# Where the DMAs of an attention and expert kernel are issued: puts of p back to SP, some loads of u to GpSimd, and the last chunk and the tails spread otherwise

## The chip, the cores and the metric

The kernel runs on one core of a Trainium2 chip. The metric is the time of one execution on the device, in microseconds (us). Engines are named as in the profile: PE (TensorE matmuls), PEld (its weight loads), DVE (VectorE), ACT (ScalarE), POOL (GpSimd), SP (SyncE, which here does nothing but issue DMAs). A "q" behind an engine's name (SPq, ACTq) is its sequencer, which waits and issues DMAs.

## The reference

Three stages over u, v (8 x 3072 x 256) and z (8 x 3072 x 64), all float32:

```python
scores = z @ z.T / 3072                   # per batch, 3072 x 3072, symmetric
attn   = maximum(scores, 0) ** 2
x      = u * (attn @ v)                   # 24576 rows of 256
h      = x @ w_in                         # 1024 wide
solu   = h * softmax(h)
ln     = (solu - mean) / sqrt(var + 1e-6) * g_ln
x2     = ln @ w_out                       # 256 wide
expert = argmax(x2 @ w_gate)              # 8 experts, one for each row
out[row] = gate * (maximum(x2 @ w1[e], 0) @ w2[e])
```

## The kernel before

**Tiling.** Each batch's 3072 rows are cut into 6 chunks of 512 rows, 48 chunks in all, and the keys of a batch into 24 blocks of 128. One *slot* is one key block of one chunk, so a chunk has 24 slots and the attention has 1152. In a slot PE multiplies one block of squared scores (128 x 512, kept as a high part `ah` and a rest `al`) with v by six matmuls into `o`. Every float32 product is made of three passes (`mm3`: L108, L109, L110).

**Symmetry.** Because the scores are symmetric, a block is computed once. Its transposed copy is written to DRAM (`kept<-sym`, `kept<-a`, L399) and fetched back when the chunk of the other side needs it (`sym<-kept`, L406: four DMAs of 64 KB for a block). So chunk 0 of a batch computes all its 24 blocks, chunk 1 20, chunk 2 16, chunk 3 12, chunks 4 and 5 8 each; the others are fetched. In chunk 5 the four blocks 16 to 19 are computed again rather than fetched. A fetched block is either transposed by DVE (`a<-sym`, L412) or read directly by ACT (`ah<-sym`, L438). ACT makes `ah`, DVE makes `al` (L443), and PE uses both. `order(j, end)` gives the order of the blocks in a chunk: the fetched ones ("old") and the others ("new") are spread evenly among each other.

**The blocks of p.** Behind the attention, each chunk has four pieces of 128 rows (t = 0..3) that go through the SoLU part in the slots of the next chunks: matmul `h`, exponential, product `p`, a 32 x 32 block transpose on DVE into `pb` (L527), then `blk_put` (L536: four DMAs of 128 KB from SBUF to the DRAM tensor `moved`), `blk_get` (L542: four DMAs that bring it back as `pT`), `blk_split` (`pth`, `ptl`), the matmuls `yp`, and `y` (L565, DVE). In each slot window of a chunk four such pieces pass. A chain of small operations (`blk_scale`, `blk_logits`, `blk_route`; mostly POOL and DVE in turn) finds each row's expert and position, and four indirect DMAs from POOL (`blk_scatter`, L659) write the rows to `sorted_rows`.

**Order.** The program is written out by hand: `at(slot, fn, ...)` puts a step into a slot, and for every slot the steps are emitted in turn. Each engine then works through its own list in that order. SP's list holds the loads of u (`load_u`, L328: two DMAs of 64 KB in each of the slots 2 to 5 of a chunk), of v and z, the fetches, the puts and gets of p, and later the experts' weights (L811) and rows (L805). In slot n, SP is given the fetch for the block of slot n + 7.

**Semaphores of DMAs.** The DMAs that SP and ACT issue share eight completion semaphores (101 to 106, 108, 109 in the trace) in the order of the program; a DMA that takes a semaphore first waits until the DMA that had it before has landed, whichever of the two engines issued that one. POOL's DMAs have eight others (111 to 118).

**Experts.** From slot 1152 on (called NS), rows are taken from `sorted_rows` in units of 512 or 256 with their expert's weights, which are split into high parts and rests (L816, L817). The units that need only the rows of the first 44 chunks begin at NS, beside the pieces of p of the last chunks. `take` gives SBUF of the attention to the experts; `split_w`, `load_w` and `load_x` prepare the first unit in the slots of the last chunk (s0 is its first slot).

In the kernel before, `blk_put` is issued from ACT when its slot lies in the window of chunk 4 or 5 of a batch (except for the last chunk's own pieces), and from SP in all others. The functions that the change touches:

Of the kernel before, what the change touches and what calls it, by code (L numbers as in the profile page):

```python
# [33 lines left out]
def attention_moe_kernel(ctx, tc, u, v, z, w_in, w_out, g_ln, w_gate, w1, w2, out):  # L34
    nc = tc.nc
# [8 lines left out]
    NCB = S // CH  # L44
    NKB = S // P
    NCHUNK = B * NCB
# [6 lines left out]
    PD = 1  # L53
    ZL = 8
    XA, XT0, XE = 2, 21, 23
    SA, SB, SC, SD, SH = 11, 14, 16, 19, 1
    TW = 8
    WS, W0, W1, W2 = 4, -11, 0, 2
    YT = 1
# [41 lines left out]
    V, A, G, T = nc.vector, nc.scalar, nc.gpsimd, nc.tensor  # L101
# [30 lines left out]
    with ExitStack() as st:  # L132
# [22 lines left out]
        def at(slot, fn, *args):  # L155
            events[slot].append((fn, args))

        def after_them(slot, fn, *args):

            events_after[slot].append((fn, args))  # L160
# [3 lines left out]
        t = vp.tile([P, 2, 4, D], F32R, tag="vw", name="raw64").bitcast(I32).rearrange("p a r d -> p (a r d)")  # L164
        raw64 = [t[:, i * 2 * CH:(i + 1) * 2 * CH].rearrange("p (f two) -> p f two", two=2) for i in range(2)]
        t = mp.tile([P, F], F32, tag="pT", name="cu64").bitcast(I32)
        c64, u64 = t[:, :CH], t[:, CH:]
        t = [mp.tile([P, CH], F32R, tag=k, name="t64").bitcast(F32) for k in ("pth0", "ptl0", "pth1", "ptl1")]
# [94 lines left out]
        z_raw, v_raw, u_raw = {}, {}, {}  # L263
        z_t, z2_t, v_t = {}, {}, {}

        def rows(x, c):
            b, j = divmod(c, NCB)
            return x[b, j * CH:(j + 1) * CH]
# [54 lines left out]
        def load_u(c, x):  # L323
            if x == 0:
                u_raw[c] = raw.tile([P, KD, CH], F32, tag="ur", name="ur")
            src = rows(u, c).rearrange("(a i) (k b j) -> k b i a j", i=32, b=4, j=32)
            for k in range(KD):
                nc.sync.dma_start(out=u_raw[c][x * 32:(x + 1) * 32, k].rearrange("i (a j) -> i a j", j=32), in_=src[k, x])  # L328

# [2 lines left out]
        def again(q, k):  # L334
            return q == NCB - 2 and k == NCB - 1
# [11 lines left out]
        t = [xrow.tile([P, KD * CH], F32, tag="x", name="sym") for _ in range(2)]  # L347
        t = [x[:, i * CH:(i + 1) * CH] for x in t for i in range(2)]
# [3 lines left out]
        def order(j, end=False):  # L352


            old = [kb for kb in range(4 * j) if end or not again(kb // 4, j)]
            new = [kb for kb in range(NKB) if kb not in old]
            return [kb for _, kb in sorted([((i + 0.5) / len(old), kb) for i, kb in enumerate(old)] +
                                           [((i + 0.5) / len(new), kb) for i, kb in enumerate(new)])]

        orders = [order(c % NCB, c == NCHUNK - 1) for c in range(NCHUNK)]  # L360

        def block(n):
# [167 lines left out]

        moved = [nc.dram_tensor(f"moved_{i}", (32, 4, F), F32, kind="Internal").ap() for i in range(4)]

        def blk_put(c, t, eng):
            w = pb_t.pop((c, t))
            for x in range(4):
                eng.dma_start(out=moved[t][:, x], in_=w[x * 32:(x + 1) * 32])  # L536

        def blk_get(c, t):
            pT_t[c, t] = w = mp.tile([P, F], F32, tag="pT", name="pT")
# [299 lines left out]
        for i in range(NU):  # L839
            w = HALF if i < N_CUT else units[i]  # L840
# [71 lines left out]
        for c in range(NCHUNK):  # L912
            b, j = divmod(c, NCB)
            s0 = c * NKB
            sb = b * NCB * NKB
            if b == 0:
                base = 4 * j - Z0
                zload = base - 5 + (j > 0)
                vload = 4 * j - V0
                at(base, turn_z, c)  # L920
            else:

                late = j >= NCB - 2
                base = sb + 3 + 4 * (j - NCB + 2) if late else sb - (NCB - 1 - j) * NKB + ZB
                zload = base - (4 if late else ZL)
                vload = sb - NKB + VL + VS * j
                at(base - 2, turn_z, c)
            at(zload, load_z, c)
            at(base, prep_z, c)
            if c > 0:  # L930
                at(s0 - LA - 5, swap_z, c)
            for h in range(2):
                step, wait = (3, 5) if b else (2, 2)
                at(vload + step * h, load_v, c, h)
                at(vload + step * h + wait, prep_v, c, h)
                at(vload + step * h + wait + (b > 0), prep_v_lo, c, h)
            for x in range(4):
                at(s0 + 2 + x, load_u, c, x)
            at(s0 + 14, turn_u, c)

            last = c == NCHUNK - 1
            more = 2 if last else 1
            s1 = s0 + NKB
            for t in range(4):
                w = s1 + 2 + (TW if last else 6) * t
                at(w, blk_h, c, t, 0)
                at(w + 1, blk_h, c, t, 1)
                at(w + 1, blk_max, c, t)
                after_them(w + 2, blk_exp, c, t)
                at(w + 3, blk_mul, c, t)  # L950
                at(w + 4, blk_turn, c, t)
                at(w + 6, blk_var, c, t)

                out_, back, cut_, y = (4, 6, 10, 12) if last else (5, 8, 12, 15) if c < NCHUNK - 2 else (5, 7, 9, 12)

                at(w + out_, blk_put, c, t, nc.scalar if (w + out_) // NKB % NCB >= NCB - 2 and not last else nc.sync)
                at(w + back, blk_get, c, t)
                cut_, y = w + cut_, w + y
                at(cut_, blk_split, c, t, 0)
                at(cut_ + 1, blk_split, c, t, 1)  # L960
                at(y, blk_y, c, t, 0)
                at(y + 1, blk_y, c, t, 1)
            e = y + 3
            for i in range(3):
                at(e + more * i, blk_scale, c, i)
            for i in range(2):
                at(e + more * (3 + i), blk_scale, c, 3)
            at(e + more * 5, blk_logits, c)
            for i in range(10):
                at(e + more * (6 + i + 2 * (i > 5)), blk_route, c, i)  # L970
            for t in range(4):
                at(e + more * (6 + 2 * t), blk_rows, c, t)
                at(e + more * (18 + 2 * t), blk_scatter, c, t)
        after = e + more * 24
        for b in range(n_in + n_out):
            for i in range(14):
# [15 lines left out]
        s0 = NS - NKB  # L992
        at(s0, take, "raw1")
        at(s0, load_w, 0, 1)
        at(s0 + 5, take, "w1h")
        at(s0 + 10, take, "w1l")
        at(s0 + 14, take, "raw2")
        at(s0 + 14, load_w, 0, 2)
        at(s0 + 19, take, "xT0")
        at(NS, take, "w2h")  # L1000
        at(NS, take, "hT")
        at(NS, take, "w2l")
# [40 lines left out]
        with tc.manual_schedule():  # L1043
            for n in range(min(lo_slot, -LA), hi_slot + 1):
                i = n + LA
                k = n - NS
# [61 lines left out]
```

## Time and profile before

| | us |
|---|---|
| median of 3 runs | 4489.14 |
| lowest and highest | 4488.82, 4499.24 |
| the profiled execution's own time | 4495.23 |
| span of the profiled execution (first to last instruction) | 4493.5 |
| PE busy, share of the span | 4293.5, 96% |
| DVE, ACT, POOL busy, share of the span | 71%, 62%, 25% |
| mean granted TensorE clock | 0.981 |

[...] In the list of waits, each row says which instruction waited for which, the total, how often and the longest. In the view by windows, each row is a stretch of time from the span's start, with the busy time of each engine in it.

### The profile page before, as it was taken

How to read it: one execution, taken by the hardware profiler on the slowest of the kernel's cores; microseconds unless marked ns; L12 is line 12 of the kernel's file. 1: busy time of each engine (PE TensorE's matmuls, PEld its weight loads, DVE VectorE, ACT ScalarE, POOL GpSimd, SP SyncE). 2: the span in 40 equal slices, each digit the busy share in tenths (PEclk: the TensorE clock that was granted, in tenths of full speed). 3: DMA queues.
4: the chain of work that ended last, by engine and by line, in shares of the span. 5: the costliest groups of instructions: out<-in, count | busy, mean ns of one | idle time of the engine just before them, and what ended most of it. 6: DMA issues, size and time to landing. Idle time of an engine off the chain costs nothing. (4 is left out here: it accounts for less than half of the span.)

```text
span 4493.5 us, 74098 instructions
## 1 busy us (share of the span) xinstructions
PE 4293.5 (96%) x23458; PEld 3701.0 (82%) x23458; DVE 3200.8 (71%) x5624; ACT 2797.7 (62%) x5184; POOL 1123.2 (25%) x2358
## 2 busy tenths in 40 slices
PE   7999998999899999999999999999789999999998
PEld 5877887888788788878877887887678999999998
DVE  8767776777687677768767776777556755666686
ACT  6756775776577577658756765875444444444565
POOL 5022222322222232222223222322122211111112
PEclk9999999999999999999999999999889999999999
DMA  5887787778778778877887887778665655555575
GB/s 151 172 154 150 182 177 137 173 175 164 140 188 176 141 177 175 162 145 181 170 151 173 171 169 143 176 168 157 119 143 141 162 141 141 141 141 142 154 214 164
DMA packets 2529034, 719.20 MB, mean 160 GB/s; under 512 B 2326653, under 2 KB 2417021, under 8 KB 2528640
## 3 DMA queue, kind: packets, MB, share of 16 engines
q1 hardware_dynamic: 2497248, 629.76, 66.7%
q0 software_dynamic: 19104, 51.15, 3.3%
q10 hardware_dynamic: 12288, 33.57, 2.8%
q8 instruction: 183, 3.00, 0.3%
q14 instruction: 211, 1.73, 0.1%
HBM read 442.46 MB, written 273.49 MB: 159 GB/s over the span
## 5 line engine op out<-in xcount | busy, mean ns | idle before, releaser
L109 PE MATMUL o<-al,vw 128*128 128x512 f32 x2304 | 931.8, 404 | 136.9 <-DVE al L443 136.4
L108 PE MATMUL o<-ah,vw 128*128 128x512 f32 x2304 | 922.6, 400 | 4.5 <-DVE ut L467 4.4
L110 PE MATMUL o<-ah,vw 128*128 128x512 f32 x2304 | 915.1, 397 | 0.0
L438 ACT ACTIVATE ah<-a 128x512 fp32r<-128x512 f32 x832 | 525.6, 632 | 199.0 <-DVE a L412 95.2
L109 PEld LDWEIGHTS o<-al,vw 128*128 128x128 f32 x2304 | 442.8, 192 | 250.8 <-DVE al L443 172.6
L428 ACT ACTIVATE r<-s 128x512 f32<-128x512 f32 x704 | 414.6, 589 | 376.8 <-PE s L423 359.3
L433 ACT ACTIVATE a<-r 128x512 f32<-128x512 f32 x704 | 438.5, 623 | 238.2 <-issue 101.6
L443 DVE TENSOR_TENSOR al<-a,ah 128x512 fp32r<-128x512 f32 x832 | 577.5, 695 | 1.2 <-ACT ah L438 0.3
L110 PEld LDWEIGHTS o<-ah,vw 128*128 128x128 f32 x2304 | 443.3, 192 | 94.4
L108 PEld LDWEIGHTS o<-ah,vw 128*128 128x128 f32 x2304 | 441.6, 192 | 91.2 <-DVE ut L467 5.9
L105 DVE TENSOR_TENSOR ptl<-pT,pth 128x512 fp32r<-128x512 f32 x384 | 264.9, 690 | 328.3 <-ACT pth L104 327.2
L108 PE MATMUL yp<-gw,pth 128*128 128x264 f32 x1536 | 445.0, 290 | 0.4 <-ACT pth L104 0.4
L109 PE MATMUL yp<-gw,pth 128*128 128x264 f32 x1536 | 443.9, 289 | 0.0
L110 PE MATMUL yp<-gw,ptl 128*128 128x264 f32 x1536 | 442.9, 288 | 0.2 <-DVE ptl L105 0.2
L865 ACT ACTIVATE zw_x<-g 128x512 fp32r<-128x512 f32 (+1 forms) x350 | 182.6, 522 | 402.9 <-PE g L110 392.4
L866 DVE SCALAR_TENSOR_TENSOR zw_x<-g,zw_x 128x512 fp32r<-128x512 f32 (+1 forms) x350 | 208.2, 595 | 266.5 <-ACT zw_x L865 261.3
L108 PEld LDWEIGHTS yp<-gw,pth 128*128 128x128 f32 x1536 | 296.3, 193 | 16.6 <-ACT pth L104 0.6
L109 PEld LDWEIGHTS yp<-gw,pth 128*128 128x128 f32 x1536 | 296.6, 193 | 15.6
L659 POOL DMA_INDIRECT sorted_rows<-y,pi x192 | 205.6, 1071 | 402.6 <-DMA sorted_rows<-y,pi 330.8
L491 PE MATMUL h<-w_in,xt 128*128 128x512 f32 x768 | 305.5, 398 | 0.0
L490 PE MATMUL h<-w_in,xt 128*128 128x512 f32 x768 | 305.3, 398 | 0.0
L110 PEld LDWEIGHTS yp<-gw,ptl 128*128 128x128 f32 x1536 | 296.0, 193 | 0.6 <-DVE ptl L105 0.6
(275 smaller groups left out, 10520.7 us busy)
## 6 DMA issues: line engine op xcount, KB each, us to landing
vw_x<-in_moe_w SPq DMA_DIRECT2D x124, 1024.0 KB
sym<-kept SPq DMA_DIRECT2D x1792, 64.0 KB
pT<-moved SPq DMA_DIRECT2D x768, 128.0 KB
kept<-sym SPq DMA_DIRECT2D x320, 256.0 KB
moved<-pb SPq DMA_DIRECT2D x512, 128.0 KB
kept<-a SPq DMA_DIRECT2D x128, 256.0 KB
moved<-pb ACTq DMA_DIRECT2D x256, 128.0 KB
vr<-in_v SPq DMA_DIRECT2D x96, 256.0 KB
```

The lines of the kernel that those rows point to most:

```text
L105: V.tensor_tensor(out=lo, in0=src, in1=hi.bitcast(F32), op=ALU.subtract)
L108: T.matmul(out=out, lhsT=lh, rhs=rh, start=start, stop=False, **kw)
L109: T.matmul(out=out, lhsT=lh, rhs=rl, start=False, stop=False, **kw)
L110: T.matmul(out=out, lhsT=ll, rhs=rh, start=False, stop=stop, **kw)
L428: A.activation(out=r, in_=s_t.pop(n), func=AF.Relu)
L433: A.activation(out=a, in_=r_t.pop(n), func=AF.Square)
L438: A.activation(out=h, in_=a_t[n], func=AF.Copy)
L443: V.tensor_tensor(out=l, in0=a_t[n], in1=ah_t[n].bitcast(F32), op=ALU.subtract)
L490: T.matmul(out=h[:, fs], lhsT=w[:, 0, kd, ts_], rhs=w_in_t[0][:, kd, fs], start=(kd == 0), stop=False)
L491: T.matmul(out=h[:, fs], lhsT=w[:, 0, kd, ts_], rhs=w_in_t[1][:, kd, fs], start=False, stop=False)
L659: G.indirect_dma_start(out=xs[:DUMMY], out_offset=bass.IndirectOffsetOnAxis(ap=pi[:, t:t + 1].bitcast(U32), axis=0), in_=y_t[c][:, t, :], ...
L866: V.scalar_tensor_tensor(out=lo, in0=h, scalar=0.0, in1=hi.bitcast(F32), op0=ALU.max, op1=ALU.subtract)
```

## The change

1. All puts of p are issued from SP, those in the windows of chunks 4 and 5 too (before: from ACT).
2. `load_u` of chunks 4 and 5 of every batch is issued from POOL's queue (before: SP).
3. In the very last chunk, `order` puts the chunk's own four blocks last, and the four blocks that are computed again are spread among the 16 fetched ones, which so take 20 slots. The steps that take over the SBUF of v and the split of the first unit's w1 (SA, SB, SC) and the load of its w2 come one or two slots later.
4. The pieces of p of chunk 45 get the shorter distances that chunk 46 had (read back 7 slots behind the start of the piece, not 8; `y` 12, not 15), and the split of both lies at 10 (chunk 45: 12, chunk 46: 9). With that, everything behind `y` comes three slots earlier for chunk 45.
5. The four scatters of chunks 45 and 46 follow one another in each slot instead of in every second one.

```diff
-    SA, SB, SC, SD, SH = 11, 14, 16, 19, 1
+    SA, SB, SC, SD, SH = 12, 15, 17, 19, 1
...
             for k in range(KD):
-                nc.sync.dma_start(out=u_raw[c][...], in_=src[k, x])
+                eng = G if c % NCB >= NCB - 2 else nc.sync
+                eng.dma_start(out=u_raw[c][...], in_=src[k, x])
...
         def order(j, end=False):
-            old = [kb for kb in range(4 * j) if end or not again(kb // 4, j)]
+            old = [kb for kb in range(4 * j) if not again(kb // 4, j)]
             new = [kb for kb in range(NKB) if kb not in old]
+            rest = new[len(new) - 4 * end:]
+            new = new[:len(new) - 4 * end]
             return [kb for _, kb in sorted([((i + 0.5) / len(old), kb) for i, kb in enumerate(old)] +
-                                           [((i + 0.5) / len(new), kb) for i, kb in enumerate(new)])]
+                                           [((i + 0.5) / len(new), kb) for i, kb in enumerate(new)])] + rest
...
-        def blk_put(c, t, eng):
+        def blk_put(c, t):
             w = pb_t.pop((c, t))
             for x in range(4):
-                eng.dma_start(out=moved[t][:, x], in_=w[x * 32:(x + 1) * 32])
+                nc.sync.dma_start(out=moved[t][:, x], in_=w[x * 32:(x + 1) * 32])
...
-                out_, back, cut_, y = (4, 6, 10, 12) if last else (5, 8, 12, 15) if c < NCHUNK - 2 else (5, 7, 9, 12)
-                at(w + out_, blk_put, c, t, nc.scalar if (w + out_) // NKB % NCB >= NCB - 2 and not last else nc.sync)
+                out_, back, cut_, y = (4, 6, 10, 12) if last else (5, 8, 12, 15) if c < NCHUNK - 3 else (5, 7, 10, 12)
+                at(w + out_, blk_put, c, t)
...
-                at(e + more * (18 + 2 * t), blk_scatter, c, t)
+                at(e + more * (18 + t * (1 if NCHUNK - 4 < c and not last else 2)), blk_scatter, c, t)
...
-        at(s0 + 5, take, "w1h")
-        at(s0 + 10, take, "w1l")
-        at(s0 + 14, take, "raw2")
-        at(s0 + 14, load_w, 0, 2)
-        at(s0 + 19, take, "xT0")
+        at(s0 + 6, take, "w1h")
+        at(s0 + 11, take, "w1l")
+        at(s0 + 16, take, "raw2")
+        at(s0 + 16, load_w, 0, 2)
+        at(s0 + 21, take, "xT0")
```

## Rows read from the trace of the kernel before

**Rows 1.** Windows: chunks 2 to 5 of one batch, one row each.
```profile
core 0: us, PE busy (x) PEld busy (x) DVE busy (x) ACT busy (x) POOL busy (x), PEclk, DMA share, GB/s
...
1360.90:1423.80 62.90, 62.90 (x322) 53.41 (x322) 51.15 (x88) 45.26 (x84) 15.41 (x42) 1.00 0.82 166
1423.80:1485.30 61.50, 61.50 (x316) 52.23 (x315) 49.85 (x86) 41.96 (x77) 15.46 (x42) 1.00 0.91 180
1485.30:1555.30 70.00, 62.32 (x308) 51.52 (x308) 43.18 (x76) 37.00 (x67) 17.18 (x42) 0.98 0.79 140
1555.30:1628.40 73.10, 65.29 (x314) 53.49 (x312) 47.80 (x83) 40.64 (x73) 22.56 (x48) 0.95 0.75 145
```

**Rows 2.** Windows: chunk 4 of all eight batches, their sum.
```profile
sum 575.30, PE 513.09 PEld 421.20 DVE 358.94 ACT 300.79 POOL 135.29; mean PE 64.14 PEld 52.65 DVE 44.87 ACT 37.60 POOL 16.91
```

**Rows 3.** Windows: chunk 5 of the first seven batches, their sum.
```profile
sum 508.40, PE 457.89 PEld 375.52 DVE 329.62 ACT 278.11 POOL 151.71; mean PE 65.41 PEld 53.65 DVE 47.09 ACT 39.73 POOL 21.67
```

**Rows 4.** Waits of PE, whole span.
```profile
PE o L109 <- DVE al L443: 136.4, 72, 9.7
PE g L108 <- DVE zw_x L866: 21.4, 5, 10.1
```

**Rows 5.** Waits of SP's queue, whole span.
```profile
SPq L536 <- DVE pb L527: 299.2, 87, 17.1
...
SPq L406 <- DMA moved<-pb: 170.1, 51, 7.5
...
SPq L328 <- DMA moved<-pb: 63.0, 15, 5.7
```

**Rows 6.** Timeline of one put in chunk 5; in brackets the idle time before and its releaser.
```profile
1574.77 1.24 DVE L527 STREAM_TRANSPOSE pb<-p 128x1024 f32<-128x1024 f32 x1
1574.80 4.21 SPq L328 DMA_DIRECT2D ur<-in_u  x2
...
1576.04 1.75 ACTq L536 DMA_DIRECT2D moved<-pb  x4
...
1577.84 0.63 ACT L433 ACTIVATE a<-r 128x512 f32<-128x512 f32 x1 [3.41 <-issue]
...
1582.94 2.15 SPq L406 DMA_DIRECT2D sym<-kept  x4
...
1584.66 0.71 DVE L412 STREAM_TRANSPOSE a<-sym 128x512 f32<-128x512 f32 x1 [8.09 <-DMA sym<-kept]
...
1586.00 0.79 PE L109 MATMUL o<-al,vw 128*128 128x512 f32 x1 [4.07 <-DVE al L443]
```

**Rows 7.** SP's issues by line: count; shortest, median, longest ns. L406: chunks 3, 4.
```profile
L542 SPq DMA_DIRECT2D pT<-moved x768: 538/663/3032, 118.1 to 3350.1; - x192
...
L536 SPq DMA_DIRECT2D moved<-pb x512: 302/420/1680, 112.3 to 3345.1; - x171
...
L406 SPq DMA_DIRECT2D sym<-kept x48: 368/487/681, 1424.2 to 1477.8; - x48
...
L406 SPq DMA_DIRECT2D sym<-kept x66: 303/487/1293, 1490.9 to 1554.9; - x66
```

**Rows 8.** POOL's indirect DMA by line, columns as in rows 7.
```profile
L659 POOL DMA_INDIRECT sorted_rows<-y,pi x192: 966/1046/1569, 234.5 to 3491.2; - x192
```

**Rows 9.** Waits of POOL, whole span.
```profile
POOL ps L649 <- DVE ps L647: 385.7, 45, 14.6
```

**Rows 10.** Windows: the last chunk, and the stretch behind it.
```profile
3154.60:3243.50 88.90, 68.20 (x306) 55.21 (x305) 46.19 (x80) 38.72 (x70) 16.08 (x39) 0.88 0.70 126
3243.50:3360.00 116.50, 93.04 (x650) 88.64 (x649) 68.70 (x143) 49.21 (x112) 29.84 (x61) 0.87 0.58 132
```

**Rows 11.** Timeline behind the last chunk: POOL, DVE and PE.
```profile
3301.44 0.98 POOL L659 DMA_INDIRECT sorted_rows<-y,pi  x1 [5.17 <-DMA sorted_rows<-y,pi]
...
3305.58 0.49 DVE L565 SCALAR_TENSOR_TENSOR y<-gw_sum,nmp,yp 128x264 f32<-128x264 f32 x1 [11.94 <-issue]
...
3306.46 0.58 PE L108 MATMUL g<-vw_x,zd_x 128*128 128x256 f32 x1 [10.13 <-DVE zw_x L866]
```

More of the change, by code (lines that the diff above doesn't have):

```diff
@@ L327, in load_u @@
             for k in range(KD):
-                nc.sync.dma_start(out=u_raw[c][x * 32:(x + 1) * 32, k].rearrange("i (a j) -> i a j", j=32), in_=src[k, x])
+                eng = G if c % NCB >= NCB - 2 else nc.sync
+                eng.dma_start(out=u_raw[c][x * 32:(x + 1) * 32, k].rearrange("i (a j) -> i a j", j=32), in_=src[k, x])
         def again(q, k):
```

## The prediction, made before the changed kernel ran

> **What bounds the kernel now.** I read the windows first, one row for each chunk of a batch [rows 1]. In chunks 2 and 3 PE is busy in every microsecond (62.90 of 62.90, 61.50 of 61.50) at full clock. Chunk 4 takes 70.0 us with 62.3 busy and chunk 5 takes 73.1 with 65.3, though they compute fewer blocks than chunk 3. Chunk 3 computes four blocks fewer than chunk 2 and is 1.4 us shorter; chunks 4 and 5 compute four fewer again, so PE alone would need about 61.5 - 1.4 = 60.1 us for each. The gap is idle time and, behind each idle stretch, matmuls at a lower granted clock (0.98 and 0.95). It is no matter of one batch: chunk 4 of the eight batches takes 575.3 us [rows 2], chunk 5 of the first seven 508.4 [rows 3], together 1083.7 us for 15 chunks, 72.2 on average. At 60.1 they would take 902, so 182 us are lost there. The last chunk is the sixteenth and is counted apart.
>
> The waits of PE say who is late: `al` from DVE, 136.4 us in 72 waits [rows 4]. The waits of SP's queue say why [rows 5]: SP stood 170.1 us before fetches (L406) and 63.0 us before loads of u (L328), each time for the landing of a put of p (`moved<-pb`). Those puts are ACT's, and the wait comes from the shared semaphores. The timeline shows one such put whole [rows 6]. DVE makes `pb` from 1574.77 on; SP's two loads of u, worth about a microsecond, last 4.21 us, because the second needs a semaphore that ACT's put took (issued from 1576.04); the fetches behind them come late; DVE idles 8.09 us for a fetched block, and PE 4.07 us for `al`. ACT pays too: 3.41 us before its next square, most of it waiting for `pb` and issuing four DMAs. Each of the two chunks has four groups of puts, and 72 waits over 16 such chunks are four to five in each.
>
> **The change part by part.**
>
> *Puts on SP.* Sixteen DMAs a chunk come to SP, 0.42 us each [rows 7], some 0.46 with the gap to the next. ACT loses them and its waits for `pb`. All DMAs of these semaphores are then SP's own, so none waits any more for one that another engine has not issued yet. New is that SP itself waits for `pb`, and that the fetches stand behind it. Whether SP can carry that is the main question, so I add up its list for chunk 4: 66 fetches [rows 7] at 2.15 / 4 = 0.54 us [rows 6] are 35.6 us, 16 puts 7.4, 16 reads of `pT` at 0.66 and a gap 11.3; together 54.3 us of the 61.5 that I shall use. Chunk 3 is the trial of it: 48 fetches [rows 7], the same puts and reads, all from SP, plus its loads of u (8 x 0.53 = 4.2) and seven or eight writes of kept blocks at a put's price (3.5) and four loads of z at a fetch's (2.1): 54.4 as well, and PE never waits there [rows 1]. Chunk 5 has four blocks' worth of loads of v and z on top, but some of its fetches are issued in chunk 4 already, and it comes out no higher. The wait for `pb`: over the span it is 299.2 us [rows 5] for 128 groups of puts, 2.3 us a group. Nothing lost is the lower bound; 4 x 2.3 = 9.3 on top of 54.3, that is 63.6 us a chunk, the upper. I take the lower, as chunk 3 is the nearest, and there SP comes to the put when `pb` is ready. Behind the put, a fetch has time until DVE's part three slots later, some 7.7 us.
>
> *Loads of u from POOL.* Eight DMAs a chunk leave SP (4.2 us, already left out above) and come to POOL's list in slots 2 to 5. [...] No row shows a direct DMA from POOL. The nearest is its indirect one of 128 rows: 1.046 us median, 966 to 1569 ns [rows 8]. A load of u has 32 x 16 pieces of 128 bytes, 512. So one costs between 1.05 us (if a DMA costs what a DMA costs) and 4.2 (if each piece does). Six stand ahead of POOL's `ps` (L649, slot 5), for which POOL now waits idle 385.7 / 45 = 8.6 us on average [rows 9]; DVE asks for `ps` a slot later, 2.6 us more. Up to 11.2 / 6 = 1.9 us each they are hidden. I take 1.5 us (nearer to the indirect DMA than to four of them): hidden, cost nothing. The load itself is needed only in slot 14.
>
> [...]
>
> *Sum for the 15 chunks.* DMA engines: chunk 4 needs 0.79 x 70.0 = 55.3 us of all sixteen, chunk 5 0.75 x 73.1 = 54.8 [rows 1]; at 61.5 us that is a share of 0.90, which chunk 3 reaches (0.91) without loss. So chunk 3's own 61.5 us is the value: 1083.7 - 15 x 61.5 = **161 us** less. Bounds: 182 (60.1 a chunk) and, with the waits of 2.3 us, 1083.7 - 15 x 63.6 = 130.
>
> *The last chunk* (88.9 us, clock 0.88 [rows 10]) has the same four puts from ACT and the same loads of u; what they cost elsewhere is 72.2 - 61.5 = 10.7 us. The new order gives the 16 fetched blocks 20 slots instead of 19; I put 2 us on it and on the later loads: **13 us**, to 76. Bounds: its DMA engines work 0.70 x 88.9 = 62.2 us, at 0.91 that is 68.4, so 20 us; nothing below.
>
> *The tails.* In the stretch behind, PE idles 21.4 us for `zw_x` [rows 4], and one wait is half of it [rows 11]: DVE stands 11.94 us before `y` of chunk 47, because its buffer still belongs to chunk 45, whose scatters POOL issues late (each waits for the one before, 5.17 us here, and for row loads that lie between them in the list); PE loses 10.13 us. The change puts these scatters at NS + 5 to 8 instead of NS + 8 to 14, all of them between the row loads at NS + 2 and NS + 10, and `y` of chunk 47 comes at NS + 14. So this wait goes, with about 2 us of slow clock [rows 10]: **12 us**. Bounds 0 and 23.5 (all idle time of the stretch, 116.5 - 93.0 [rows 10]).
>
> The profiled execution took 4495.2 us (span 4493.5). 4495.2 - 161 - 13 - 12 = 4309. The median of the runs lies 6 us below the profiled one, so I predict **4303 us**.
>
> **The rivals.**
>
> *A, the DMA engines don't follow.* Chunks 4 and 5 would run at the share of chunk 2, 0.82, rather than 0.91: 55.3 / 0.82 = 67.4 and 54.8 / 0.82 = 66.8 us, 1083.7 - 15 x 67.1 = 77 us saved; with half of the last two terms (12) the median would be 4400. For it: the fetches are many pieces of 128 bytes, and fetches that wait behind other DMAs come later. Against it: chunk 3. [...] The row of chunk 3 and the waits of SP say that issue time is what is short here.
>
> *B, POOL becomes the bound (slower).* A load of u costs 4.2 us: six are 25.2, `ps` comes 14.0 us late, DVE stands before L652 with all its later work, and a chunk takes 61.5 + 14.0 = 75.5. 15 x 75.5 - 1083.7 = 49 us more, less 25 from the last terms: 4513. It decides from 1.9 us on, and cancels the gain at (11.2 + 10.7) / 6 = 3.65 us. [...]
>
> *C, the waits only change their name.* The landing of fetches holds DVE anyway, with SP standing at `pb` instead of at a semaphore. Then only the tail's 12 us are left: 4477, within what I call the same. Against it: chunks 0 to 3, where SP waits for `pb` and PE doesn't wait.
>
> **How the numbers follow.** Forecast 0.68, A 0.19, C 0.04, B 0.09. The predicted time is the forecast's. Its own range is 4264 (182 + 20 + 23 saved) to 4345 (130, 13 and nothing). The range that should hold the time takes in A: 4268 to 4405. C and B and a little of the ends stay outside. A difference of 0.3% (13 us) is about what can be told from no change: faster 0.87, same 0.04, slower 0.09.
>
> **What would show it.** Right: chunks 4 and 5 at 60 to 64 us with clock near 1.00; no wait of SP for `moved<-pb` at L406 or L328 in them, instead some for `pb` at L536; `al` as a cause of PE's waits down from 136 us to about 30; ACT's 3.4 us gaps gone; loads of u on POOL under 1.9 us each, and no wait of DVE L652 for `ps`; DVE's 11.9 us before `y` gone. Wrong: DVE L652 waiting for POOL in each of these chunks (B); DMA share stuck at about 0.82 with DVE still waiting for `sym<-kept` (A); SP's wait at L536 at 3 us or more a group with PE still stopping four times a chunk (C).

## The result and the profile after

The changed kernel takes 4314.03 us (median of 4 runs, 4313.29 to 4316.04); the kernel before, on the same chip, 4489.48. The ratio is 0.9605, with a 95% interval of 0.9588 to 0.9622. The profiled execution took 4313.29 us, its span is 4311.6 us against 4493.5, and the mean granted clock (the share of its full speed that the profile lists as granted to TensorE) rose from 0.981 to 0.995. In the code of after, lines behind the change are shifted: the fetch is L410, the put L540, `al` L447, the load of u L330, the scatter L663.

Windows of the same batch, chunks 2 to 5, of the kernel after; they answer to [rows 1].

```profile
1297.10:1359.98 62.88, 62.88 (x323) 53.38 (x321) 51.15 (x89) 45.24 (x84) 15.36 (x42) 1.00 0.80 164
1359.98:1421.49 61.51, 61.51 (x316) 52.26 (x315) 50.05 (x87) 42.02 (x77) 15.69 (x42) 1.00 0.90 176
1421.49:1482.42 60.93, 60.15 (x309) 50.65 (x307) 43.27 (x76) 37.20 (x67) 21.67 (x50) 1.00 0.90 161
1482.42:1545.43 63.01, 62.03 (x313) 51.66 (x313) 47.35 (x83) 40.77 (x73) 27.74 (x56) 1.00 0.98 169
```

The sums over chunk 4 of eight batches and over chunk 5 of the first seven, in that order [rows 2, 3], then the last chunk and the stretch behind it [rows 10]:

```profile
sum 484.22, PE 479.41 PEld 405.08 DVE 353.26 ACT 298.54 POOL 168.57; mean PE 59.93 PEld 50.63 DVE 44.16 ACT 37.32 POOL 21.07
...
sum 445.15, PE 435.74 PEld 360.81 DVE 333.58 ACT 284.30 POOL 193.26; mean PE 62.25 PEld 51.54 DVE 47.65 ACT 40.61 POOL 27.61
...
3001.95:3077.45 75.50, 65.46 (x305) 53.06 (x305) 47.16 (x84) 37.42 (x68) 21.07 (x54) 0.91 0.84 150
...
3077.40:3193.00 115.60, 100.82 (x761) 96.27 (x760) 76.11 (x157) 55.31 (x126) 33.06 (x66) 0.97 0.67 157
```

Chunks 2 and 3 are what they were. Chunks 4 and 5 have lost nearly all their idle time, and their clock is at 1.00. The 15 chunks come to 484.2 + 445.2 = 929.4 us, 154.3 less; the last chunk is 13.4 shorter; all that is left of the span (4311.6 - 929.4 - 75.5 = 3306.7, before 3320.9) is 14.2 shorter. Together that is the 181.9 us of the span.

The waits of the whole span, of PE [rows 4], of SP's queue [rows 5] and of POOL [rows 9]:

```profile
PE o L109 <- DVE al L447: 26.0, 28, 3.8
PE yp L108 <- ACT pth L104: 13.5, 4, 5.9
...
PE g L108 <- DVE zw_x L870: 6.9, 3, 2.8
...
SPq L540 <- DVE pb L531: 300.1, 88, 12.9
...
SPq L546 <- DMA moved<-pb: 21.4, 29, 2.0
...
POOL ps L653 <- DVE ps L651: 254.6, 45, 12.2
```

The wait for `al` fell from 136.4 to 26.0 us. No row for the landing of a put is left at the fetch or at the load of u; what is left, 21.4 us, is at the read of `pT`, which needs the put's data. SP's standing at `pb` is the same in total (300.1 against 299.2 us) though it now issues 192 groups instead of 128: in chunks 4 and 5 it hardly stands there (no row for it in the two windows of this batch).

The loads of u by the engine that issues them: count; shortest, median, longest ns.

```profile
L330 SPq DMA_DIRECT2D ur<-in_u x256: 316/487/2280, 31.8 to 2893.0; - x128
L330 POOL DMA_DIRECT2D ur<-in_u x128: 648/666/773, 286.2 to 3016.0; - x128
```

And SP's queue in chunk 5 of the same batch: start, duration, line, operation, number of DMAs.

```profile
1499.32 0.78 SPq L305 DMA_DIRECT2D vr<-in_v  x1
1500.14 4.62 SPq L410 DMA_DIRECT2D sym<-kept  x8
1504.85 1.84 SPq L540 DMA_DIRECT2D moved<-pb  x4
1506.79 0.42 SPq L305 DMA_DIRECT2D vr<-in_v  x1
1507.26 5.82 SPq L410 DMA_DIRECT2D sym<-kept  x8
1513.18 2.83 SPq L546 DMA_DIRECT2D pT<-moved  x4
1516.10 0.92 SPq L305 DMA_DIRECT2D vr<-in_v  x1
```

Each row begins 0.04 to 0.10 us behind the end of the one before: in this stretch SP waits for nothing. In the whole chunk no wait of SP is longer than 1.2 us; its list is nearly full.

### The profile page after: what moved, and what is told of

It is laid out like the page before. It is cut to its first block, busy times and chain, and to the rows that moved or that the text cites. A ratio compares the mean times of both kernels' runs of the same rounds, so it can differ in the third digit from the quotient of the medians.

```text
span 4311.6 us, 74509 instructions
## 1 busy us (share of the span) xinstructions
PE 4231.3 (98%) x23458; PEld 3664.3 (85%) x23458; DVE 3197.2 (74%) x5624; ACT 2800.7 (65%) x5184; POOL 1200.7 (28%) x2486
## 4 chain that ended last, share of the span: by engine, by line
PE 75%; DMA 7%; SPq 7%; DVE 6%; issue 2%; ACT 2%; POOL 0%; DVEq 0%; POOLq 0%; ACTq 0%
PE o L109 10%; PE o L108 10%; PE o L110 9%; SPq L410 4%; PE y L109 3%; PE y L108 3%; PE y L110 3%; PE g L108 3%; PE yp L108 3%; PE g L109 3%; PE yp L110 3%; PE yp L109 3%; PE h L494 3%; PE h L495 3%; PE h L498 3%; PE g L110 3%
## 5 line engine op out<-in xcount | busy, mean ns | idle before, releaser
L109 PE MATMUL o<-al,vw 128*128 128x512 f32 x2304 | 912.8, 396 | 26.6 <-DVE al L447 26.0
L108 PE MATMUL o<-ah,vw 128*128 128x512 f32 x2304 | 910.4, 395 | 3.0 <-DVE ut L471 2.8
L110 PE MATMUL o<-ah,vw 128*128 128x512 f32 x2304 | 900.7, 391 | 0.0
L447 DVE TENSOR_TENSOR al<-a,ah 128x512 fp32r<-128x512 f32 x832 | 575.5, 692 | 1.0
L109 PEld LDWEIGHTS o<-al,vw 128*128 128x128 f32 x2304 | 434.6, 189 | 122.0 <-DVE al L447 44.1
L110 PEld LDWEIGHTS o<-ah,vw 128*128 128x128 f32 x2304 | 434.9, 189 | 93.8
L108 PEld LDWEIGHTS o<-ah,vw 128*128 128x128 f32 x2304 | 434.7, 189 | 88.0 <-issue 2.7
L108 PE MATMUL yp<-gw,pth 128*128 128x264 f32 x1536 | 440.1, 286 | 13.5 <-ACT pth L104 13.5
L109 PE MATMUL yp<-gw,pth 128*128 128x264 f32 x1536 | 438.5, 285 | 0.0
L663 POOL DMA_INDIRECT sorted_rows<-y,pi x192 | 206.5, 1076 | 426.0 <-DMA sorted_rows<-y,pi 375.4
L104 ACT ACTIVATE pth<-pT 128x512 fp32r<-128x512 f32 x384 | 237.8, 619 | 123.4 <-DMA pT<-moved 123.3
L108 PEld LDWEIGHTS yp<-gw,pth 128*128 128x128 f32 x1536 | 289.7, 189 | 30.2 <-ACT pth L104 15.5
L109 PEld LDWEIGHTS yp<-gw,pth 128*128 128x128 f32 x1536 | 290.7, 189 | 14.4
```

The source lines that it names most:

```text
L104: A.activation(out=hi, in_=src, func=AF.Copy)
L108: T.matmul(out=out, lhsT=lh, rhs=rh, start=start, stop=False, **kw)
L109: T.matmul(out=out, lhsT=lh, rhs=rl, start=False, stop=False, **kw)
L110: T.matmul(out=out, lhsT=ll, rhs=rh, start=False, stop=stop, **kw)
L447: V.tensor_tensor(out=l, in0=a_t[n], in1=ah_t[n].bitcast(F32), op=ALU.subtract)
```

## The experiments

The first four runs take the change apart. They were to tell apart two theories. By S, SP's list sets the pace, by its issue time and its waits for ACT's puts, so that the loads of u count by themselves and the puts alone bring only a part. By R, `al` is late because ACT stands at `pb` and issues the puts, so that the puts are nearly the whole loss and the loads alone bring nothing. The later ones ask how the puts cost what they cost: by SP's waits for the semaphores, or by ACT's standing. The table has all kernels; the ratio is to the kernel before on the same chip. The stretches are those of the profiled span, in us: the 15 chunks (sums of windows as above), the last chunk, and the rest of the span. They come from one execution each. Among the kernels with the same code in the rest of the span (after, 6, 9 to 12) it ranges from 3301.5 to 3310.3, so a difference of a few us there says little.

| kernel | median us | ratio to before (95%) | 15 chunks | last | rest |
|---|---|---|---|---|---|
| before (runs beside after) | 4489.48 | 1 | 1083.7 | 88.9 | 3320.9 |
| after | 4314.03 | 0.9605 (0.9588 to 0.9622) | 929.4 | 75.5 | 3306.7 |
| 1 puts on SP alone | 4354.45 | 0.9708 (0.9692 to 0.9725) | 948.4 | 85.0 | 3318.7 |
| 2 u from POOL alone | 4484.44 | 0.9995 (0.9985 to 1.0005) | 1079.5 | 85.6 | 3321.0 |
| 3 both | 4329.07 | 0.9651 (0.9635 to 0.9667) | 921.8 | 81.6 | 3321.1 |
| 4 parts 3 to 5 alone | 4467.49 | 0.9957 (0.9944 to 0.9970) | 1073.0 | 84.3 | 3306.7 |
| 5 after without 4 and 5 | 4331.19 | 0.9648 (0.9632 to 0.9664) | 926.9 | 81.2 | 3321.7 |
| 6 after, ACT stands at pb | 4311.33 | 0.9608 (0.9592 to 0.9624) | 929.9 | 75.9 | 3304.5 |
| 7 before, ACT's puts a slot later | 4331.26 | 0.9653 (0.9637 to 0.9669) | 924.0 | 83.6 | 3318.2 |
| 8 before, a slot sooner | 4607.65 | 1.0262 (1.0245 to 1.0279) | 1196.9 | 88.9 | 3324.2 |
| 9 after, eight more issues of SP | 4437.98 | 0.9882 (0.9864 to 0.9900) | 1057.4 | 75.9 | 3310.3 |
| 10 after, more bytes | 4324.34 | 0.9638 (0.9622 to 0.9654) | 938.9 | 75.8 | 3301.5 |
| 11 after, puts from POOL | 4292.80 | 0.9566 (0.9550 to 0.9582) | 906.9 | 76.1 | 3308.0 |
| 12 after, ACT's puts a slot later | 4300.72 | 0.9582 (0.9566 to 0.9598) | 913.5 | 77.5 | 3307.2 |

**1. The puts alone**, in the kernel before.

```diff
-at(w + out_, blk_put, c, t, nc.scalar if (w + out_) // NKB % NCB >= NCB - 2 and not last else nc.sync)
+at(w + out_, blk_put, c, t, nc.sync)
```

> The kernel before with one part alone: all puts of p from SP, u still from SP. Theory S (SP's list sets the pace: issue time plus its waits for puts that ACT issues): the waits go, but SP's list is 4.2 us a chunk longer than in the changed kernel, where it is already full (chunk 4: 55.2 us of issues plus some 4 of gaps in 59.7). So chunks 4 and 5 at 63.5 to 67, 4314 + 15 x 4 + 25 for the tails = about 4400, between 4370 and 4420. Rival R (ACT's standing at pb and its issue time is what makes al late): ACT is as free as in the changed kernel, so 4335 to 4350, all of the gain but the tails.

131 us less than before on the same chip (4485.46): 4 us above the range of R and 16 below that of S. The puts are three quarters of the whole gain, although SP got 16 issues more in each of these chunks. PE's wait for `al` (136.4 us before [rows 4]) is

```profile
PE o L109 <- DVE al L443: 57.8, 41, 12.8
```

**2. The loads of u alone**, in the kernel before.

```diff
-nc.sync.dma_start(out=u_raw[c][...], in_=src[k, x])
+(G if c % NCB >= NCB - 2 else nc.sync).dma_start(out=u_raw[c][...], in_=src[k, x])
```

> The kernel before with the other part alone: u of chunks 4 and 5 from POOL, puts there still from ACT. Theory S: SP saves 4.2 us a chunk but still stands for ACT's puts (13 to 15 us a chunk), so chunks 4 and 5 at about 68 to 70, 4489 - 15 x 3 = 4430 to 4460. Rival R: ACT is held as before, 4480 to 4490.

No difference from before, as R has it. The wait didn't go with the loads; SP now comes sooner to the fetch, and waits there (170.1 us in [rows 5], the loads' own 63.0 gone), and PE waits for `al` as before:

```profile
SPq L406 <- DMA moved<-pb: 245.4, 76, 8.8
...
PE o L109 <- DVE al L443: 138.6, 53, 9.8
```

Both 1 and 2 miss the ranges of S, and 2 lies in that of R. But taking the puts from ACT removes both ACT's standing and the shared semaphores, so which of them cost the time is left to 6 to 8.

**3. Both.**

The edit is that of 1 and of 2 together.

> Both parts on DMA queues, without the new order of the last chunk and without the tails. Both theories: chunks 4 and 5 as in the changed kernel, the last chunk partly, the tail as before: 4314 + 16 for the tail + 0 to 13 for the last chunk = 4328 to 4345. If puts and u only help together, e1 and e2 fall short of it by much: their gains add to less than this one's.

As expected. On top of the puts the loads are worth 26.6 us in the 15 chunks, alone 4.

**4. Parts 3 to 5 alone**: the changed kernel with the edits of 1 and 2 taken back.

```diff
-eng = G if c % NCB >= NCB - 2 else nc.sync
+eng = nc.sync
...
-at(w + out_, blk_put, c, t)
+at(w + out_, blk_put, c, t, nc.scalar if (w + out_) // NKB % NCB >= NCB - 2 and not last else nc.sync)
```

> The kernel before with the rest alone: order of the last chunk, later takeovers, tails of chunks 45 and 46; puts and u as before. Tail 16 us less, the last chunk 0 to 8 less: 4489 - 16 to 24 = 4465 to 4473. If the last chunk's gain of 13 us in the changed kernel came from the order alone, 4460.

As expected: 18 us less than before.

**5. Parts 4 and 5 taken back**, to see which of the three does it.

```diff
-... (5, 8, 12, 15) if c < NCHUNK - 3 else (5, 7, 10, 12)
+... (5, 8, 12, 15) if c < NCHUNK - 2 else (5, 7, 9, 12)
...
-at(e + more * (18 + t * (1 if NCHUNK - 4 < c and not last else 2)), blk_scatter, c, t)
+at(e + more * (18 + 2 * t), blk_scatter, c, t)
```

> The changed kernel without its parts 4 and 5: the pieces of chunks 45 and 46 and their scatters stand where the kernel before has them; the order of the last chunk (part 3), the puts and the loads of u as changed. If the tail's gain is the wait of DVE before y of chunk 47, it comes back: 4323 to 4330 us. If it is part 3's, nothing changes: 4310 to 4318.

4331 us, a microsecond above the range of the wait of DVE, and what experiment 3 has without any of the three: part 3, the new order of the last chunk with its later loads, is worth nothing that shows without the other two. Parts 4 and 5 are worth 17 us. With them undone DVE's wait before `y` is there again, and PE's for `zw_x` (here 6.9 us in after); DVE's rows are of the end of the span, PE's of all of it:

```profile
DVE y L569 <- issue: 11.9, 2, 11.3
...
PE g L108 <- DVE zw_x L870: 19.9, 4, 9.5
```

**6. ACT stands at `pb`, and issues nothing**: the changed kernel, with three ACTIVATEs of `pb` into a tile that nobody reads, where ACT's puts had been.

```diff
+idle_t = mp.tile([P, CH], F32, tag="idle", name="idle")
...
-def blk_put(c, t):
+def blk_put(c, t, stand):
     w = pb_t.pop((c, t))
+    for i in range(3 * stand):
+        A.activation(out=idle_t, in_=w[:, (i % 2) * CH:(i % 2 + 1) * CH], func=AF.Copy)
...
-at(w + out_, blk_put, c, t)
+at(w + out_, blk_put, c, t, (w + out_) // NKB % NCB >= NCB - 2 and not last)
```

> The changed kernel, with extra work on ACT: at the place in its list where the kernel before has a put of p (windows of chunks 4 and 5) ACT reads pb three times into a tile that nobody uses (three ACTIVATEs of 128x512, about 0.6 us each). So ACT waits for pb as before and is then held about as long as by four issues, but it issues no DMA and no semaphore is shared. If the loss came from SP's waits for semaphores that ACT's puts held (the prediction's reading), 4314 to 4335 us. If it came from ACT, whose squares for the next blocks came 3.4 us late, most of the 161 us comes back: 4400 to 4480.

Nothing changed against after (ratio 0.9608 for 0.9605), and standing of this length is out as the cause: ACT does stand at `pb`, and PE waits no more than in after. Added up from the trace, ACT's idle time ahead of these 64 places is 94 us, against 121 us ahead of the 64 groups of puts in before.

```profile
ACT idle L541 <- DVE pb L532: 93.9, 55, 2.4
...
PE o L109 <- DVE al L447: 24.9, 24, 3.6
```

**7. The puts stay on ACT, one slot later** in the program, in the kernel before.

```diff
+on_act = (w + out_) // NKB % NCB >= NCB - 2 and not last
-at(w + out_, blk_put, c, t, nc.scalar if ...)
+at(w + out_ + on_act, blk_put, c, t, nc.scalar if ...)
```

> The kernel before, with the puts that ACT issues one slot later in the program (the reads of pT stay where they are). pb is then ready when ACT comes to the put, so that ACT only loses the issue time of 1.75 us, not the wait ahead of it; the semaphores are shared as before. If ACT's standing is what counted, about half of the loss goes: 4400 to 4440 us. If SP's waits for the semaphores counted, SP waits as before, since the DMAs that follow the put still need its landing: 4465 to 4495.

Neither range held, and that of the semaphores, the prediction's reading, is the farther off: 4331 us, as good as experiment 3, with puts on ACT, loads of u on SP and shared semaphores. SP's waits for the puts' landing had not stayed. At the fetch and at the read of `pT` they are now

```profile
SPq L542 <- DMA moved<-pb: 48.3, 27, 11.5
...
SPq L406 <- DMA moved<-pb: 39.8, 37, 4.2
```

and 5.5 us at the load of u; in before it was 170.1 at the fetch and 63.0 at the load of u [rows 5]. PE's wait for `al` is as small as in after:

```profile
PE o L109 <- DVE al L443: 27.6, 28, 3.7
```

This edit moves the puts in ACT's list too, and there ACT no longer stands at `pb`. Since that standing was free in 6, what is left is the place of the put among SP's DMAs. By the semaphores in the trace of before, the DMA that takes a put's semaphore next is a fetch of SP's for 212 of the 256 puts, and a load of u for 15. A slot later, the DMAs of SP that take the put's semaphores stand a slot farther on in SP's own list, and by the time SP gets there most puts have landed. That this is how it works is argued from 6 and 7; no run gave ACT's puts semaphores of their own.

**8. The puts on ACT, one slot sooner**, to see whether the place works in the other direction too.

```diff
+on_act = (w + out_) // NKB % NCB >= NCB - 2 and not last
-at(w + out_, blk_put, c, t, nc.scalar if ...)
+at(w + out_ - on_act, blk_put, c, t, nc.scalar if ...)
```

> The kernel before, with the puts that ACT issues one slot earlier in the program, right behind the transpose that makes pb. Four fetches fewer then stand on SP's list ahead of the DMAs that take the puts' semaphores; the put itself can't come sooner than pb. If the loss is the loop from ACT's standing at pb over the shared semaphore to SP's fetches, SP needs the landing a slot (2.6 us) sooner and the waits grow: 4520 to 4640 us. If only the making of pb sets the time of the put, and the place in the program doesn't matter, 4475 to 4500.

It does: 118 us slower than before, within the range of the loop over the shared semaphores.

```profile
SPq L542 <- DMA moved<-pb: 193.6, 40, 10.3
...
SPq L328 <- DMA moved<-pb: 90.6, 15, 9.7
...
SPq L406 <- DMA moved<-pb: 70.7, 12, 7.1
...
PE o L109 <- DVE al L443: 212.5, 75, 10.0
```

Over all its lines SP now waits 400 us for landings of puts (with 45.0 before writes of kept blocks); in the kernel before it was 297, the two of [rows 5] and

```profile
SPq L399 <- DMA moved<-pb: 43.1, 7, 7.1
SPq L542 <- DMA moved<-pb: 20.6, 10, 10.3
```

A slot later it was 94. The times go with them: 4608, 4489, 4331. But in this kernel ACT stands longer as well: ahead of its puts it is idle 270 us in all (121 in before, 94 in 6), and it waits for landings, 98.8 us ahead of its next L428. Experiment 6 tested no standing of that length, so how much of the 118 us is SP's isn't shown.

**9. Eight issues more on SP, without bytes**: the changed kernel, with 8 DMAs of 128 bytes from z into a DRAM tensor that nobody reads in each chunk 4 and 5 of seven batches.

```diff
+def more_issues(c, x):
+    for k in range(2):
+        nc.sync.dma_start(out=sink[2 * x + k, 0:1, 0], in_=z[0, 2 * x + k:2 * x + k + 1, 0:32])
...
+                if j >= NCB - 2 and b < B - 1:
+                    at(s0 + 2 + 5 * x, more_issues, c, x)
```

> The changed kernel, with more to do for SP and next to nothing for the DMA engines: in chunks 4 and 5 of the first seven batches SP issues eight more DMAs of 128 bytes each, two at a time, from z into a DRAM tensor that nobody reads. By the median of a put that is 8 x 0.42 = 3.4 us of SP a chunk. The eight loads of u, 4.2 us of SP, made 1.8 us a chunk between the two earlier experiments with the puts on SP. If SP's issue time is what holds chunk 5 (and nearly chunk 4), 1.5 to 3 us more in each of 14 chunks: 4335 to 4356 us. If it isn't, 4312 to 4320.

The sign was right and the size far off: 124 us more than after, about 9 in each of 14 chunks instead of 1.5 to 3. SP's queue in chunk 4 shows why:

```profile
1501.08 1.83 SPq L546 DMA_DIRECT2D moved<-pb  x4
1502.95 1.17 SPq L358 DMA_DIRECT2D sink<-in_z  x2
1504.16 6.53 SPq L416 DMA_DIRECT2D sym<-kept  x8
1510.79 2.81 SPq L552 DMA_DIRECT2D pT<-moved  x4
1513.64 6.07 SPq L416 DMA_DIRECT2D sym<-kept  x8
1519.75 1.16 SPq L358 DMA_DIRECT2D sink<-in_z  x2
```

It has no gap, as in after; but these two groups of eight fetches take 6.5 and 6.1 us, where medians of 0.49 us with gaps make 4.2. I added up SP's issues in chunk 4 over the first seven batches, with a gap of 0.043 us behind each: in after 55.3 us for 96 issues, with gaps 59.4, in a chunk of 60.1 on average; here 66.8 for 107, with gaps 71.4, in a chunk of 73.1. So SP's list sets the chunk here; in after it is nearly as long as the chunk, in which PE is busy for 59.9 us too. The new issues are some 5 of the 12 us; three more of the other issues fall into the longer chunk, and about 6 us are single issues of over 0.9 us, which became more and longer (8.6 a chunk for 5.6). What makes an issue long is not settled here.

**10. More bytes, without issues of SP**: the changed kernel, with 8 more copies of 64 KB from u into an unused DRAM tensor, issued by POOL, in the same chunks.

```diff
+def more_bytes(c, x):
...
+    for k in range(2):
+        G.dma_start(out=sink[2 * x + k + 8 * (c % 2)], in_=src[k, x])
...
+                if j >= NCB - 2 and b < B - 1:
+                    at(s0 + 2 + 5 * x, more_bytes, c, x)
```

> The changed kernel, with more to do for the DMA engines and nothing for SP: in chunks 4 and 5 of the first seven batches POOL issues eight more copies of 64 KB each, in pieces of 128 bytes, from u into a DRAM tensor that nobody reads. 8 x 512 pieces at about 15 ns on 16 engines are 3.8 us a chunk. If chunk 5 is held by the DMA engines (a share of 0.98 of them busy), its seven chunks become 3 to 5 us longer and chunk 4 (0.92) 0 to 2: 4335 to 4362 us. If SP's issue time holds it, 4312 to 4322.

Between the two expectations: 4324 us, 10 more than after, 0.6 in each of the 15 chunks on average, chunk 5 from 63.6 to 64.4, far from 3 to 5 (a piece of 128 bytes takes 13 ns in the median in the trace of before, near the 15 of the estimate). The DMA engines' share of 0.98 in chunk 5 of after is no limit; experiment 11 has 1.02 without an idle microsecond of PE.

**11. The puts of chunks 4 and 5 from POOL**, in the changed kernel, which takes 16 issues from SP and shares no semaphore.

```diff
-at(w + out_, blk_put, c, t)
+at(w + out_, blk_put, c, t, G if (w + out_) // NKB % NCB >= NCB - 2 and not last else nc.sync)
```

> The changed kernel, with the puts of p in the windows of chunks 4 and 5 issued from POOL (SP in all others, and for the last chunk's own pieces). ACT doesn't stand at pb, no semaphore is shared with SP, and SP loses 16 issues of 0.42 us in each of these chunks. If SP's issue time is what still holds chunks 5 (63 us against 60), 4285 to 4305 us. If it is the sixteen DMA engines, which have the same to do, 4308 to 4320. If POOL's standing at pb and its own issue time hold up ps and what hangs on it, 4325 or more.

4293 us, the range of SP's issue time: faster than the change by 0.4% (the intervals don't touch). Chunks 4 and 5 of the same batch, and POOL's puts in chunk 5:

```profile
1410.64:1470.35 59.71, 59.71 (x309) 50.76 (x307) 45.48 (x78) 38.15 (x69) 30.71 (x66) 1.00 1.02 172
1470.35:1531.41 61.06, 61.06 (x315) 51.88 (x313) 49.62 (x83) 40.10 (x73) 34.33 (x72) 1.00 0.95 171
...
L540 POOL DMA_DIRECT2D moved<-pb x16: 492/498/612, 1473.7 to 1519.8; - x16
```

PE is busy in every microsecond. These two numbers are what the chunks need of PE alone.

**12. The puts on ACT a slot later, in the changed kernel** (loads of u from POOL).

```diff
-at(w + out_, blk_put, c, t)
+on_act = (w + out_) // NKB % NCB >= NCB - 2 and not last
+at(w + out_ + on_act, blk_put, c, t, nc.scalar if on_act else nc.sync)
```

> The changed kernel, with the puts in the windows of chunks 4 and 5 issued from ACT again, but one slot later than the kernel before had them. SP then has neither puts nor loads of u in these chunks, and the shared semaphores are there. If the place in ACT's list was the whole trouble, chunks 4 and 5 come to 60 to 61 us as with the puts on POOL: 4288 to 4302 us. If the shared semaphores still cost something, it stays at 4305 to 4325.

4301 us, in the lower range, near its upper end; SP still waits 46.6 us at the fetch and 54.0 at the read of `pT` for landings of puts, and the 15 chunks are 6.6 us longer than in 11. So the place in the lists was nearly the whole trouble. Whether the little that is left comes from the shared semaphores or from ACT's issue time isn't told apart.

## Why the prediction was right, point by point

- **The loss is in chunks 4 and 5, and comes over the shared semaphores.** That the puts on ACT at that place cost the time is shown (1, 7, 11). That it comes over the semaphores is well supported: ACT's standing without a DMA costs nothing (6), and moving the puts a slot each way takes SP's waits for landings from 297 to 94 or to 400 us, and the time with them (7, 8; in 8 ACT's longer standing has a part that isn't known). The prediction also counted ACT's 3.41 us [rows 6] as paid; in 6 a standing of that kind cost nothing. What it didn't see is that the put need not leave ACT for this. Nor were matmuls slow behind each idle stretch: in the batch of [rows 1] L109 took 0.79 us behind 3.35 and 4.07 us without work, in stretches (1496 to 1500 and 1584.8 to 1592) with a clock of 0.57 and 0.53, but 0.49 and 0.50 us at 1.00 behind 1.20 and 2.15 us.
- **The 15 chunks: -161, measured -154.3**, 62.0 us a chunk for 61.5. PE alone needs 59.7 and 61.1 (11), 60.4 on average, where the prediction had 60.1.
- **SP carries the puts.** It does, with less to spare than worked out. The list was put at 54.3 us of 61.5; with gaps it is 59.4 of 60.1 in chunk 4, and in chunk 5, which was to be no higher, 60.5 of 63.6. The term that was mis-sized is the duration of an issue: the sum took medians, and these held, but in chunk 4 the issues of over 0.9 us rose from 3.0 to 5.6 a chunk, in chunk 5 from 3.4 to 7.1, and their excess over 0.45 us from 2.2 and 2.7 to 5.0 and 6.8. That SP's list held chunk 5 at 63.6 is shown by 11 and 12: with 16 issues taken from SP it comes to 61.1 and 61.6. Comparing with chunk 3 gave the right answer because chunk 3 is nearly full as well: added up in the same way from the trace of before, its list is 58.1 us of 61.5, where the prediction had 54.4.
- **SP's wait for `pb`: nothing taken of 2.3 us.** Right; in chunks 4 and 5 SP comes late enough to find `pb` ready.
- **Loads of u from POOL: 1.5 us each, hidden.** 0.67 us, under the lower bound of 1.05, hidden as said: POOL still waits 254.6 us for DVE at `ps`. B is out. The issues range from 648 to 773 ns, with DVE busy for 73% of chunks 4 and 75% of chunks 5. The value of the loads, though, hangs on the puts: alone they bring nothing (2), with the puts on SP 25 us (1, 3), as SP is then nearly full.
- **A, the DMA engines don't follow**: they do, to a share of 0.98, and 1.02 in 11. The loads' move to another issuing engine was worth 25 us where issue time was short (3) and nothing where it wasn't (2). No run shows which of the DMA engines a queue's packets take. **C** is out by 1 and by the waits of PE.
- **The last chunk: -13, measured -13.4, by other causes.** The prediction gave about 11 to the puts and the loads, and 2 to the order. By the table the puts gave 3.9 (1), the loads 3.4 (3), the order with its later loads 0.4 (5), and parts 4 and 5 the last 5.7 (5 to after). These parts are differences of single executions. The total was right by luck.
- **The tails: -12, measured -14.2.** The wait that was named is gone, and it comes back with parts 4 and 5 undone, with 15 us in the rest of the span (5). Against it stands chunk 46, which these parts make longer (60.0 us in 5, 63.8 in after); that cost was not in the sum.

The sum missed by 11 us (4303 for 4314). The 15 chunks gave 6.7 us less than forecast, the last chunk and the tails 2.6 more; and the median, put 6 us below the profiled execution, lies 0.7 above it, which makes the other 6.7.

Open is what makes single issues of SP long. What POOL issues beside them doesn't explain it alone: issues of over 0.9 us in chunks 4 and 5 are 3.7 and 3.6 a chunk (7) or 4.6 and 5.6 (1) with no DMA from POOL beside the scatters. With 8 loads from POOL they are 3.7 and 3.1 (2), 5.6 and 7.1 (after), 6.6 and 10.4 (6) or 8.6 and 9.0 (9); with 16 DMAs 7.1 and 10.3 (10), with 24 8.0 and 8.7 (11).

## What to carry to other kernels

Where two queues take completion semaphores in turn, a DMA that comes late on one can hold the other (here SP stood 170.1 us before fetches and 63.0 before loads of u [rows 5]), and, as argued in 7, how far on in the other's list the same semaphore is needed can decide: try a later place for the late DMA before moving it to another queue (here a slot was worth 156 us). Before moving DMAs for issue time, add up the queue's issues in that stage, from the trace and not from medians. Here eight loads less on SP brought nothing while SP stood waiting, and 1.8 us a chunk when its list was nearly full; eight small DMAs more on the full list cost 9. And test parts alone and together, since the loads of u were worth 0 or 25 us depending on where the puts were.

## What the runs showed of the hardware that was not expected

A direct DMA of 512 pieces of 128 bytes takes POOL 0.67 us to issue and SP 0.49; a put takes POOL 0.50 and SP 0.42. The indirect one of 128 rows, 1.05 us [rows 8], was no lower bound. The profile's DMA share reached 1.02 in chunk 4 of 11 without PE losing anything, so a share near 1 was no limit here; since it passes 1, it is not a plain share of busy time. Chunk 5 was held up instead by a queue whose instructions only issue (63.6 us a chunk in after, 61.1 in 11, with 16 issues fewer on it). An issue of SP's, 0.42 us in the median for a put and 0.66 for a read of `pT`, can take far longer: up to 3.0 us for such a read [rows 7], and 2.6 us for a DMA of 128 bytes in 9 (521 to 2624 ns).
